# The skip and gated spectral rows of a fused FFT and state-space kernel: summed in fp32 by ScalarE and an accumulating DMA

## The chip, the cores and the metric

The kernel runs on one core of a Trainium2 chip. Its time is the device time of one execution in microseconds (us). Before the change it is 354.18 us, the median of four runs (354.07 to 355.04).

## What is computed

Two branches read the same x (2048 x 1024, bf16), and a gate of each row mixes them:

```python
x = A_x
g = sigmoid((x * gate_w).sum(-1, keepdims=True))
a = irfft2(rfft2(x) * (w_r + 1j * w_i))            # spectral branch, cast to bf16
# state-space branch: complex diagonal scan over the 2048 rows
h_t = Lam_bar * h_(t-1) + x_t @ B_bar.T
b = 2 * real(h @ C.T) + x * Dskip
out = g * a + (1 - g) * b
```

## The kernel before

**Stages.** The program has three stretches. First, up to about 110 us, comes the forward transform: `fstage` folds x, `fd` makes the transform along a row, `bf_w` the one over the rows and the product with the weights W, and `bi` starts the way back. There are 16 groups g. Then, to about 160 us, comes the inverse: `idm` (16 tiles, into yp), the folding of yp into pm on VectorE (L635, L636), and `fi`, whose result ya is stored in a DRAM scratch, `ya_scratch`. The last stage makes the output, 16 tiles of 128 rows, tb = 0 to 15.

**The state-space branch** runs through all of it in 16 units (c, q): c is one of four chunks of 512 time steps, q one of four groups of 256 states. Unit number n is 4c + q. For a unit, TensorE (PE) makes 4 x 8 products of x with B into the PSUM tile psu (L388, two buffers), ScalarE (ACT) scales each psu into the tile u (L390, two buffers), and VectorE (DVE) rotates u by tables (L399, L401, L403), runs four scans (L408), computes the carry (L417 to L421) and rotates back (L425, L427), where L427 writes into u again. L429 writes the state tile h. The h of c = 0 and 3 lies in a pool, the others in the arrays `big` and `xT` that are free by then.

**The last stage** (`half`, `c_all`): for tile tb and half dh of its columns, 16 products of h with C into the PSUM tile psy (L770, three buffers of a whole tile). All four h of chunk tb // 4 are needed. For the first eleven tiles, a 17th product with the identity matrix adds the skip row xc = x * Dskip (L774), and DVE forms out = psy * (1 - g) + gac (L779), where gac is the spectral row scaled by g on ACT (L760). For the last five tiles, ACT writes (1 - g) * xc as fp32 into xf (L763), DVE adds gac to it (L764), and L779 takes xf instead of gac. The loads of xc and gac and the store of o are issued on SyncE (SP).

**What sets the order.** `ssm_all`, `fft_main` and `c_all` are generators with a cost in us for each step. A loop takes the next step of the branch that is behind: L718 paces the units against the transform (20 by the end of the forward part, 42 at the end of the inverse), L722 and L792 let the units run to 42 and 43 before the last stage, and L797 paces them against `c_all` with a factor of 1.02. Within that program order a scheduler places the instructions of PE, DVE and ACT. SP and POOL follow the written order up to `order1.close()` (L748); after it they are scheduled too. POOL issues only the loads of W, L239, 14 pairs of them; it has no work after 110 us. `gates` computes g: 32 small products, a sigmoid on ACT and three small DVE operations, begun beside the fifth pm (jj == 4).

Of the kernel before, what the change touches and what calls it, by code (L numbers as in the profile page):

```python
# [20 lines left out]
D = 1024  # L21
K = 512
P = 128
# [113 lines left out]
def kernel(  # L137
# [256 lines left out]
    def ssm_dve(c, q, u):  # L394
        tq = tab[:, 2 * q:2 * q + 2]
        full = [P, 2, 2, TC]
        cu = rp.tile(full, BF16, name="cu", tag="cu")
        su = rp.tile(full, BF16, name="su", tag="su")
        nc.vector.tensor_mul(out=cu, in0=u, in1=tq[:, :, 0:1, :].to_broadcast(full))  # L399
        yield  # L400
        nc.vector.tensor_mul(out=su, in0=u[:, :, ::-1, :], in1=tq[:, :, 1:3, :])  # L401
        yield
        nc.vector.tensor_add(out=cu, in0=cu, in1=su)  # L403
        yield
        for jj in range(2):
            jb = 2 * q + jj
            for ri in range(2):
                nc.vector.tensor_tensor_scan(out=su[:, jj, ri, :], data0=r_sb[:, jb:jb + 1].to_broadcast([P, TC]),  # L408
                                             data1=cu[:, jj, ri, :],
                                             initial=(0.0 if c == 0 else carry[q][:, jj, ri:ri + 1]),  # L410
                                             op0=ALU.mult, op1=ALU.add)
                if not (jj and ri):
                    yield
        if c + 1 < NCH:
            ge = su[:, :, :, TC - 1]
            k1 = sm.tile([P, 2, 2], FP32, name="k1")
            nc.vector.tensor_mul(out=k1, in0=ge, in1=cTC[:, 2 * q:2 * q + 2].unsqueeze(2).to_broadcast([P, 2, 2]))  # L417
            k2 = sm.tile([P, 2, 2], FP32, name="k2")
            nc.vector.tensor_mul(out=k2, in0=ge[:, :, ::-1], in1=sg[:, 2 * q:2 * q + 2, :])
            cy = sm.tile([P, 2, 2], FP32, name=f"carry{q}")  # L420
            nc.vector.tensor_add(out=cy, in0=k1, in1=k2)  # L421
            carry[q] = cy
        yield
        h = h_tile(c, q)
        nc.vector.tensor_mul(out=cu, in0=su, in1=tq[:, :, 0:1, ::-1].to_broadcast(full))  # L425
        yield
        nc.vector.tensor_mul(out=u, in0=su[:, :, ::-1, :], in1=tq[:, :, 1:3, ::-1])  # L427
        yield
        nc.vector.tensor_add(out=h, in0=cu, in1=u)  # L429
        hs[c, q] = h  # L430
        yield


# [62 lines left out]
    def bf_w(g):  # L496
        X1 = X1s.pop(g)
        M = MM[g]
        Mr, Mi, Mn = M[:, 0, :], M[:, 1, :], M[:, 2, :]
        Im, Re, ORe, OIm = X1[:, 0:256], X1[:, 256:512], X1[:, 512:768], X1[:, 768:1024]  # L500
        X = Xtiles[g % 2]
        pe = psF.tile([P, 2, 512], FP32, name="ps_xe", tag="ps")
        kw = dict(skip_group_check=True)
        nc.tensor.matmul(pe[:, 0, 0:256], lhsT=Mr, rhs=Re, start=True, stop=False, **kw)
        nc.tensor.matmul(pe[:, 0, 1:257], lhsT=Mi, rhs=Im, start=False, stop=True, **kw)
        nc.tensor.matmul(pe[:, 1, 0:256], lhsT=Mn, rhs=Re, start=True, stop=False, **kw)
        nc.tensor.matmul(pe[:, 1, 1:257], lhsT=Mr, rhs=Im, start=False, stop=True, **kw)
        nc.scalar.copy(out=X[:, :, 0:513:2], in_=pe[:, :, 0:257])
        po = psF.tile([P, 2, 256], FP32, name="ps_xo", tag="ps")
        nc.tensor.matmul(po[:, 0, :], lhsT=Mr, rhs=ORe, start=True, stop=False)  # L510
        nc.tensor.matmul(po[:, 0, :], lhsT=Mi, rhs=OIm, start=False, stop=True)
        nc.tensor.matmul(po[:, 1, :], lhsT=Mn, rhs=ORe, start=True, stop=False)
        nc.tensor.matmul(po[:, 1, :], lhsT=Mr, rhs=OIm, start=False, stop=True)
        (nc.vector.tensor_copy if g < 3 else nc.scalar.copy)(out=X[:, :, 1:513:2], in_=po)  # L514
        W = WT[g]
        Y = fr.tile([P, 2, 514], BF16, name="Y")
        t2 = gc1.tile([P, 2, 514], BF16, name="t2")
        nc.vector.tensor_mul(out=Y, in0=X, in1=W[:, 0:1, :].to_broadcast([P, 2, 514]))  # L518
        nc.vector.tensor_mul(out=t2, in0=X, in1=W[:, 1:2, :].to_broadcast([P, 2, 514]))
        nc.vector.tensor_sub(out=Y[:, 0, :], in0=Y[:, 0, :], in1=t2[:, 1, :])  # L520
        nc.vector.tensor_add(out=Y[:, 1, :], in0=Y[:, 1, :], in1=t2[:, 0, :])
        Ys[g] = Y
        if g + 2 < 16:
            load_W(g + 2)
# [78 lines left out]
    def fft_main():  # L603
# [24 lines left out]
        for jj in range(9):  # L628
            if jj < 8:
                yp = fr.tile([P, 2, 2, 512], BF16, name="yp")  # L630
                for jl in range(2):
                    idm(2 * jj + jl, yp[:, jl])
                    yield 1.1
                pm = fr.tile([P, 2, 2, 512], BF16, name="pm")
                nc.vector.tensor_add(out=pm[:, :, 0, :], in0=yp[:, :, 0, :], in1=yp[:, :, 1, :])  # L635
                nc.vector.tensor_sub(out=pm[:, :, 1, :], in0=yp[:, :, 0, :], in1=yp[:, :, 1, :])  # L636
                pms[jj] = pm
                if jj == 4:
                    gt = gates()
                    next(gt)  # L640
                    yield 2.0
                if jj == 4 + 1:
                    next(gt)
                    yield 0.3
            if jj > 0:
# [69 lines left out]
    ssm = Gen(ssm_all())  # L715
    fft = Gen(fft_main())
    while not fft.done:
        if ssm.t < (20 * (fft.t - 3.5) / (54.4 - 3.5) if fft.t < 54.4 else 20 + (42 - 20) * (fft.t - 54.4) / 35.0):  # L718
            ssm.step()
        else:  # L720
            fft.step()
    while ssm.t < 42:  # L722
        ssm.step()
    fctx.close()

    with ExitStack() as bctx:
# [5 lines left out]
        xcs, gacs = {}, {}  # L732

        def load_xc(tb):
            xcs[tb] = fin.tile([P, D], BF16, name="xc", bufs=3)
            nc.sync.dma_start(out=xcs[tb], in_=x[P * tb:P * (tb + 1), :])

        def load_gac(tb):
            gacs[tb] = fin.tile([P, D], BF16, name="gac", bufs=4)
            nc.sync.dma_start(out=gacs[tb], in_=ya_dram[P * tb:P * (tb + 1), :])  # L740

        for tb in range(3):
            load_xc(tb)
        load_gac(0)
        load_gac(1)
        load_C(1)
        load_gac(2)
        order1.close()  # L748

        psys = {}  # L750

        def half(tb, dh):
            c, tq = tb // 4, tb % 4
            if dh == 0:
                psys[tb] = psY.tile([P, D], FP32, name="psy", tag="psy")
            psy, xc, gac = psys[tb], xcs[tb], gacs[tb]
            if dh == 0:
                nc.vector.tensor_mul(out=xc, in0=xc, in1=dsk_bc)
            else:
                nc.scalar.activation(out=gac, in_=gac, func=ACT.Copy, scale=gf[:, tb:tb + 1])  # L760
                if tb >= 11:
                    xf = rp.tile([P, D], FP32, name="xf", tag="cu")
                    nc.scalar.activation(out=xf, in_=xc, func=ACT.Copy, scale=om_f[:, tb:tb + 1])  # L763
                    nc.vector.tensor_add(out=xf, in0=xf, in1=gac)  # L764
                    gac = xf
            ds = slice(512 * dh, 512 * (dh + 1))
            i = 0
            for jb in range(8):
                for ri in range(2):
                    nc.tensor.matmul(psy[:, ds], lhsT=hs[c, jb // 2][:, jb % 2, ri, P * tq:P * (tq + 1)],  # L770
                                     rhs=CT[dh][:, jb, ri, :], start=(i == 0), stop=(i == 15 and tb >= 11))
                    i += 1
            if tb < 11:
                nc.tensor.matmul(psy[:, ds], lhsT=ident, rhs=xc[:, ds], start=False, stop=True)  # L774
            if dh == 0:
                return
            o = fin.tile([P, D], BF16, name="o")
            for ds in ((slice(0, D),) if tb < 15 else (slice(0, 512), slice(512, D))):
                nc.vector.scalar_tensor_tensor(out=o[:, ds], in0=psy[:, ds], scalar=om_f[:, tb:tb + 1], in1=gac[:, ds],  # L779
                                               op0=ALU.mult, op1=ALU.add)  # L780
                nc.sync.dma_start(out=out2[P * tb:P * (tb + 1), ds], in_=o[:, ds])

        def c_all():
            order = [(0, 0), (1, 0), (2, 0), (0, 1), (1, 1), (2, 1)] + [(tb, dh) for tb in range(3, 16) for dh in range(2)]
            for tb, dh in order:
                if dh == 0 and 3 <= tb + 1 < 16:
                    load_xc(tb + 1)
                    load_gac(tb + 1)
                half(tb, dh)
                yield 3.6  # L790

        while ssm.t < 43:  # L792
            ssm.step()
        cg = Gen(c_all())
        t0 = ssm.t
        while not cg.done:
            if not ssm.done and ssm.t - t0 <= cg.t * 1.02:  # L797
                ssm.step()
            else:
                cg.step()  # L800
# [30 lines left out]
```

## Time and profile before

| what | value |
|---|---|
| median of four runs | 354.18 us |
| the profiled execution: its own time | 355.03 us |
| the profiled execution: span from first to last instruction | 353.2 us |
| granted TensorE clock, mean | 0.995 |
| busy in the span: PE, DVE, ACT, POOL | 93%, 86%, 50%, 8% |
| bytes moved by DMA, mean rate | 42.91 MB, 121 GB/s |
| L770, psy products | 512, 379 ns each in the record |
| L388, psu products | 512, 379 ns each in the record |
| L774, identity products | 22, 379 ns each in the record |
| L779, DVE o, whole tile | 15, 1.27 to 1.28 us each |

The records of matmuls overlap, since they are pipelined: a product of 512 columns has a record of 379 ns, but the next one starts 0.216 us later. The span is divided by stage in the tables that follow. "Idle before" is the time in which an engine stood before an instruction, with the event that released it. An instruction that issues a DMA is shown on the queue of its engine (SPq, POOLq); "to landing" is the time from issue to the arrival of the data.

### The profile page before, as it was taken

Reading aid. Unit: us, or ns where it says so; the run is one execution under the profiler, and the core shown is the slowest. Engines: PE = TensorE matmul, PEld = TensorE weight load, DVE = VectorE, ACT = ScalarE, POOL = GpSimd, SP = SyncE. Lnnn points to the kernel's source line nnn. Section 1 sums busy time; section 2 is a strip of 40 time slices with the busy share of each in tenths; the row PEclk is TensorE's granted clock in tenths of the full one; section 3 lists DMA queues with packets and bytes.
Section 4 is the critical chain, followed back from the end, with each engine's and each line's share of the span. In section 5 each row is a group of like instructions: output and inputs, shape, how many; then the busy total and the mean of one; then the engine's idle time right before and its main releaser. Section 6 shows DMA issues by size and latency. Waiting matters only on the chain.

```text
span 353.2 us, 4881 instructions
## 1 busy us (share of the span) xinstructions
PE 329.7 (93%) x1826; PEld 175.0 (50%) x1826; DVE 302.3 (86%) x423; ACT 177.9 (50%) x245; POOL 27.9 (8%) x73
## 2 busy tenths in 40 slices
PE   3888989899799999989799999999999999999995
PEld 1675656566456556544344444444444444444442
DVE  4998749979978989895969999999999999999431
ACT  1998879779679786883323322322313223223110
POOL 5330321222110000000000000000000000000000
PEclk9999999999989999999999999999999999999999
DMA  7999997989979130214991340211201303142101
GB/s 271 343 138 220 180 256 178 165 212 199 138 166 202 62 119 32 89 67 151 235 203 37 104 114 16 89 32 59 89 30 62 89 0 91 60 119 88 63 31 58
DMA packets 65864, 42.91 MB, mean 121 GB/s; under 512 B 52400, under 2 KB 55472, under 8 KB 65840
## 3 DMA queue, kind: packets, MB, share of 16 engines
q1 hardware_dynamic: 64144, 38.75, 45.4%
q0 software_dynamic: 1344, 3.68, 4.5%
q8 instruction: 14, 0.23, 0.3%
q10 hardware_dynamic: 352, 0.17, 0.2%
q14 instruction: 10, 0.08, 0.1%
HBM read 21.61 MB, written 8.39 MB: 85 GB/s over the span
## 4 chain that ended last, share of the span: by engine, by line
PE 64%; issue 13%; DMA 10%; DVE 8%; POOL 3%; ACT 1%; SPq 0%; DVEq 0%; POOLq 0%; ACTq 0%
PE psy L770 30%; PE psu L388 23%; DMA W<-in_A_w_r_dram 4%; PE ps_id L550 3%; DMA W<-in_A_w_i_dram 2%; POOL W L239 2%; DVE su L408 2%; DMA CT<-in_A_x_dram 1%; PE psy L774 1%; DMA xt<-in_A_x_dram 1%; DMA xc<-in_A_x_dram 1%; PE ps_q L539 1%; PE ps_y L569 1%; PE ps_q L540 1%; PE ps_y L572 1%
## 5 line engine op out<-in xcount | busy, mean ns | idle before, releaser
L388 PE MATMUL psu<-xT,BT 128*128 128x512 bf16 x512 | 120.4, 379 | 1.1 <-DMA xT<-in_A_x_dram 1.1
L388 PEld LDWEIGHTS <-BT 128*128 128x128 bf16 x512 | 49.6, 98 | 57.8 <-issue 3.7
L408 DVE TENSOR_TENSOR_SCAN su<-r_sb,carry,cu 128x512 bf16<-128x512 f32 x48 | 57.8, 1264 | 0.4
L390 ACT ACTIVATE u<-psu,nrho 128x512 bf16<-128x512 f32 x32 | 22.0, 688 | 56.6 <-PE psu L388 56.6
L770 PEld LDWEIGHTS <-h 128*128 128x128 bf16 x256 | 25.0, 98 | 30.4 <-issue 0.3
L390 ACT ACTIVATE u<-psu,rho 128x512 bf16<-128x512 f32 x32 | 22.3, 696 | 33.1 <-PE psu L388 33.0
L760 ACT ACTIVATE gac<-gac,gf 128x1024 bf16<-128x1024 bf16 x16 | 18.3, 1147 | 33.4 <-DMA gac<-ya_scratch 30.6
L399 DVE TENSOR_TENSOR cu<-u,tab 128x2048 bf16<-128x2048 bf16 x16 | 19.8, 1237 | 13.8 <-ACT u L390 13.7
L770 PE MATMUL psy<-CT,h 128*128 128x512 bf16 x128 | 28.9, 379 | 0.0
L770 PE MATMUL psy<-big,h 128*128 128x512 bf16 x128 | 28.9, 379 | 0.0
L543 ACT CAST big<-ps_q 128x1024 bf16<-128x1024 f32 x16 | 16.6, 1035 | 9.8 <-PE ps_q L542 9.6
L770 PEld LDWEIGHTS <-big 128*128 128x128 bf16 x128 | 12.5, 98 | 15.1
L770 PEld LDWEIGHTS <-xT 128*128 128x128 bf16 x128 | 12.5, 98 | 15.1
L539 PE MATMUL ps_q<-MM,Y 128*128 128x256 bf16 x64 | 15.7, 281 | 4.5 <-DVE Y L520 4.3
L403 DVE TENSOR_TENSOR cu<-cu,su 128x2048 bf16<-128x2048 bf16 x16 | 19.5, 1219 | 0.2
L481 PE MATMUL ps_d<-G_sb,big 128*128 128x256 bf16 (+3 forms) x128 | 19.6, 294 | 0.0
L425 DVE TENSOR_TENSOR cu<-su,tab 128x2048 bf16<-128x2048 bf16 x16 | 19.5, 1218 | 0.1
L401 DVE TENSOR_TENSOR su<-u,tab 128x2048 bf16<-128x2048 bf16 x16 | 19.5, 1217 | 0.0
L427 DVE TENSOR_TENSOR u<-su,tab 128x2048 bf16<-128x2048 bf16 x16 | 19.5, 1216 | 0.0
L518 DVE TENSOR_TENSOR Y<-X,W 128x1028 bf16<-128x1028 bf16 x16 | 11.0, 688 | 9.3 <-ACT X L514 7.9
L408 DVE TENSOR_TENSOR_SCAN su<-r_sb,cu 128x512 bf16<-128x512 f32 x16 | 18.9, 1210 | 0.1
L465 PE MATMUL ps_f<-BT,eo 128*128 128x256 bf16 x64 | 16.4, 297 | 2.4 <-DVE big L470 1.3
(171 smaller groups left out, 547.7 us busy)
## 6 DMA issues: line engine op xcount, KB each, us to landing
ya_scratch<-ya SPq DMA_DIRECT2D x16, 256.0 KB, 2.0
xc<-in_A_x_dram SPq DMA_DIRECT2D x16, 256.0 KB, 2.6
gac<-ya_scratch SPq DMA_DIRECT2D x16, 256.0 KB, 2.7
out_dram<-o SPq DMA_DIRECT2D x15, 256.0 KB, 2.0
MM<-c_MM SPq DMA_DIRECT2D x16, 192.0 KB, 3.9
xt<-in_A_x_dram SPq DMA_DIRECT2D x4, 512.0 KB, 4.4
CT<-in_A_x_dram SPq DMA_DIRECT2D x4, 512.0 KB, 7.7
W<-in_A_w_r_dram POOLq DMA_DIRECT2D x14, 128.2 KB, 4.3
```

Of the source, the lines that this page charges most:

```text
L388: nc.tensor.matmul(psu, lhsT=BT[:, jb, ri, dblk, :], rhs=xT[:, dblk, TC * c:TC * (c + 1)], start=(dblk == 0), stop=(dblk == 7))
L390: nc.scalar.activation(out=u[:, jj, ri, :], in_=psu, func=ACT.Copy, scale=(nrho if ri else rho)[:, jb:jb + 1])
L399: nc.vector.tensor_mul(out=cu, in0=u, in1=tq[:, :, 0:1, :].to_broadcast(full))
L401: nc.vector.tensor_mul(out=su, in0=u[:, :, ::-1, :], in1=tq[:, :, 1:3, :])
L403: nc.vector.tensor_add(out=cu, in0=cu, in1=su)
L408: nc.vector.tensor_tensor_scan(out=su[:, jj, ri, :], data0=r_sb[:, jb:jb + 1].to_broadcast([P, TC]), data1=cu[:, jj, ri, :], initial=(0.0 ...
L425: nc.vector.tensor_mul(out=cu, in0=su, in1=tq[:, :, 0:1, ::-1].to_broadcast(full))
L427: nc.vector.tensor_mul(out=u, in0=su[:, :, ::-1, :], in1=tq[:, :, 1:3, ::-1])
L481: nc.tensor.matmul(ps[:, lo:lo + w], lhsT=FX[:, q, 8 * g:8 * g + 8, :], rhs=G_sb[:, o:o + w], start=start, stop=stop, skip_group_check=True)
L539: nc.tensor.matmul(dst, lhsT=Yr[:, e:e + 255:2], rhs=ri_, start=True, stop=False, **kw)
L760: nc.scalar.activation(out=gac, in_=gac, func=ACT.Copy, scale=gf[:, tb:tb + 1])
L770: nc.tensor.matmul(psy[:, ds], lhsT=hs[c, jb // 2][:, jb % 2, ri, P * tq:P * (tq + 1)], rhs=CT[dh][:, jb, ri, :], start=(i == 0), stop=(i ...
```

## The change

In the last stage every tile now takes the fp32 way, and the sum of the two rows is made by a DMA:

- `prep_d(tb)`: DVE multiplies xc by Dskip, as before.
- `prep_a(tb)`: ACT scales gac by g, and writes xf = (1 - g) * xc in fp32 (three buffers). A DMA issued on POOL adds the bf16 row gac to the fp32 row xf. Then SP issues the loads of xc and gac for tile tb + 2.
- `half`: 16 products only, for every tile; L774 and the DVE add L764 are gone. The last step reads xf.
- A table `pre` says after which half each `prep_d` and `prep_a` is written.
- xc has two buffers in place of three and gac three in place of four, and two tiles in place of three are loaded ahead.
- ACT and SP keep their written order in the last stage, where the scheduler placed them before.

Four other things change. The copy of ps_xo into X (L514) is on DVE for four groups in place of three. `gates` begins one pm later. The pace of the units is 18.5 and 44 in place of 20 and 42, then 44 and 48 in place of 42 and 43, and the factor 1.05 in place of 1.02. A branch `if False` is added to `ssm_dve`, which is never taken.

```diff
-        (nc.vector.tensor_copy if g < 3 else nc.scalar.copy)(out=X[:, :, 1:513:2], in_=po)
+        (nc.vector.tensor_copy if g < 4 else nc.scalar.copy)(out=X[:, :, 1:513:2], in_=po)
...
-                if jj == 4:
+                if jj == 5:
                     gt = gates()
                     next(gt)
                     yield 2.0
-                if jj == 4 + 1:
+                if jj == 5 + 1:
...
-        if ssm.t < (20 * (fft.t - 3.5) / (54.4 - 3.5) if fft.t < 54.4 else 20 + (42 - 20) * (fft.t - 54.4) / 35.0):
+        if ssm.t < (18.5 * (fft.t - 3.5) / (54.4 - 3.5) if fft.t < 54.4 else 18.5 + (44 - 18.5) * (fft.t - 54.4) / 35.0):
...
-    while ssm.t < 42:
+    while ssm.t < 44:
...
-        for tb in range(3):
+        for tb in range(2):
             load_xc(tb)
-        load_gac(0)
-        load_gac(1)
+            load_gac(tb)
         load_C(1)
-        load_gac(2)
         order1.close()
-
-        psys = {}
+        if ('Activation','SP'):
+            bctx.enter_context(tc.manual_schedule(engines=set(getattr(mybir.EngineType, e) for e in ('Activation','SP'))))
+
+        psys, xfs = {}, {}
+
+        def prep_d(tb):
+            nc.vector.tensor_mul(out=xcs[tb], in0=xcs[tb], in1=dsk_bc)
+
+        def prep_a(tb):
+            xc, gac = xcs.pop(tb), gacs.pop(tb)
+            nc.scalar.activation(out=gac, in_=gac, func=ACT.Copy, scale=gf[:, tb:tb + 1])
+            xf = fin.tile([P, D], FP32, name="xf", bufs=3)
+            nc.scalar.activation(out=xf, in_=xc, func=ACT.Copy, scale=om_f[:, tb:tb + 1])
+            nc.gpsimd.dma_start(out=xf, in_=gac, accum_op=ALU.add)
+            xfs[tb] = xf
+            if tb + 2 < 16:
+                load_xc(tb + 2)
+                load_gac(tb + 2)
 
         def half(tb, dh):
...
-            if dh == 0:
-                nc.vector.tensor_mul(out=xc, in0=xc, in1=dsk_bc)
-            else:
-                nc.scalar.activation(out=gac, in_=gac, func=ACT.Copy, scale=gf[:, tb:tb + 1])
-                if tb >= 11:
-                    xf = rp.tile([P, D], FP32, name="xf", tag="cu")
-                    nc.scalar.activation(out=xf, in_=xc, func=ACT.Copy, scale=om_f[:, tb:tb + 1])
-                    nc.vector.tensor_add(out=xf, in0=xf, in1=gac)
-                    gac = xf
...
-                                     rhs=CT[dh][:, jb, ri, :], start=(i == 0), stop=(i == 15 and tb >= 11))
+                                     rhs=CT[dh][:, jb, ri, :], start=(i == 0), stop=(i == 15))
                     i += 1
-            if tb < 11:
-                nc.tensor.matmul(psy[:, ds], lhsT=ident, rhs=xc[:, ds], start=False, stop=True)
...
-                nc.vector.scalar_tensor_tensor(out=o[:, ds], in0=psy[:, ds], scalar=om_f[:, tb:tb + 1], in1=gac[:, ds],
-                                               op0=ALU.mult, op1=ALU.add)
+                nc.vector.scalar_tensor_tensor(out=o[:, ds], in0=psy[:, ds], scalar=om_f[:, tb:tb + 1],
+                                               in1=xfs[tb][:, ds], op0=ALU.mult, op1=ALU.add)
...
         def c_all():
             order = [(0, 0), (1, 0), (2, 0), (0, 1), (1, 1), (2, 1)] + [(tb, dh) for tb in range(3, 16) for dh in range(2)]
+            pre = {(0, 0): [(prep_d, 0), (prep_d, 1)], (1, 0): [(prep_a, 0)], (2, 0): [(prep_a, 1)],
+                   (0, 1): [(prep_d, 2)], (1, 1): [(prep_a, 2)], (2, 1): [(prep_d, 3)], (3, 0): [(prep_a, 3), (prep_d, 4)],
+                   (3, 1): [(prep_a, 4)]}
+            for n in range(5, 16):
+                pre[n - 1, 0] = [(prep_d, n)]
+                pre[n - 1, 1] = [(prep_a, n)]
             for tb, dh in order:
-                if dh == 0 and 3 <= tb + 1 < 16:
-                    load_xc(tb + 1)
-                    load_gac(tb + 1)
                 half(tb, dh)
+                for f, n in pre.get((tb, dh), ()):
+                    f(n)
                 yield 3.6
 
-        while ssm.t < 43:
+        while ssm.t < 48:
             ssm.step()
...
-            if not ssm.done and ssm.t - t0 <= cg.t * 1.02:
+            if not ssm.done and ssm.t - t0 <= cg.t * 1.05:
```

More of the change, by code (lines that the diff above doesn't have):

```diff
@@ L424, in ssm_dve @@
         h = h_tile(c, q)
+        hs[c, q] = h
+        if False:
+            nc.vector.tensor_mul(out=h, in0=su, in1=tq[:, :, 0:1, ::-1].to_broadcast(full))
+            yield
+            nc.vector.tensor_mul(out=cu, in0=su[:, :, ::-1, :], in1=tq[:, :, 1:3, ::-1])
+            nc.gpsimd.dma_start(out=h, in_=cu, accum_op=ALU.add)
+            yield
+            return
         nc.vector.tensor_mul(out=cu, in0=su, in1=tq[:, :, 0:1, ::-1].to_broadcast(full))
@@ L429, in ssm_dve @@
         nc.vector.tensor_add(out=h, in0=cu, in1=u)
-        hs[c, q] = h
         yield
@@ L734, in load_xc @@
         def load_xc(tb):
-            xcs[tb] = fin.tile([P, D], BF16, name="xc", bufs=3)
+            xcs[tb] = fin.tile([P, D], BF16, name="xc", bufs=2)
             nc.sync.dma_start(out=xcs[tb], in_=x[P * tb:P * (tb + 1), :])
         def load_gac(tb):
-            gacs[tb] = fin.tile([P, D], BF16, name="gac", bufs=4)
+            gacs[tb] = fin.tile([P, D], BF16, name="gac", bufs=3)
             nc.sync.dma_start(out=gacs[tb], in_=ya_dram[P * tb:P * (tb + 1), :])
-        for tb in range(3):
+        for tb in range(2):
             load_xc(tb)
-        load_gac(0)
-        load_gac(1)
+            load_gac(tb)
         load_C(1)
-        load_gac(2)
         order1.close()
-        psys = {}
+        if ('Activation','SP'):
[13 more added lines that the diff above has]
+                load_gac(tb + 2)
         def half(tb, dh):
@@ L755, in half @@
                 psys[tb] = psY.tile([P, D], FP32, name="psy", tag="psy")
-            psy, xc, gac = psys[tb], xcs[tb], gacs[tb]
-            if dh == 0:
-                nc.vector.tensor_mul(out=xc, in0=xc, in1=dsk_bc)
-            else:
-                nc.scalar.activation(out=gac, in_=gac, func=ACT.Copy, scale=gf[:, tb:tb + 1])
-                if tb >= 11:
-                    xf = rp.tile([P, D], FP32, name="xf", tag="cu")
-                    nc.scalar.activation(out=xf, in_=xc, func=ACT.Copy, scale=om_f[:, tb:tb + 1])
-                    nc.vector.tensor_add(out=xf, in0=xf, in1=gac)
-                    gac = xf
+            psy = psys[tb]
             ds = slice(512 * dh, 512 * (dh + 1))
```

## The prediction

> **What bounds the kernel now.** I read the busy time by stretch first, then the chain of work that ended last, then VectorE's timeline, because TensorE (PE) and VectorE (DVE) are both near full and only the order of their work tells which one decides.
>
> ```profile
> 28.80:110.20 81.40, 74.67 (x515) 46.83 (x516) 67.17 (x109) 65.75 (x84) 17.38 (x29) 0.98 1.01 190
> 110.20:160.40 50.20, 49.19 (x314) 29.82 (x314) 45.48 (x59) 39.50 (x59) 0.00 (x0) 1.00 0.29 91
> 160.40:172.20 11.80, 9.65 (x45) 4.26 (x44) 9.10 (x9) 3.71 (x7) 0.00 (x0) 1.00 0.67 187
> 172.20:321.30 149.10, 149.10 (x692) 67.53 (x692) 143.26 (x148) 43.28 (x54) 0.00 (x0) 1.00 0.29 78
> 321.30:349.10 27.80, 27.76 (x129) 12.41 (x127) 12.93 (x14) 5.63 (x5) 0.00 (x0) 1.00 0.15 53
> ```
>
> The columns are length, then busy time of PE, weight loads, DVE, ACT, POOL, then clock and DMA. From 172.2 to the end PE has no gap at all. DVE is 96% busy until 321.3 and only then loose; ACT is 29% busy and POOL unused. So in the last stage a matmul taken away is time gained, but only as long as DVE, close behind, can follow.
>
> ```profile
> 170.24 1.26 DVE su L408
> 171.50 0.59 DVE xc L758
> 172.13 0.38 PE psy L774
> ...
> 314.53 34.55 PE psy L770 x160
> 349.10 0.75 DVE o L779
> ```
>
> The chain shows the one hole of this stage: the first identity product (L774) waits for the skip row xc, which waits for its load and for a scan in DVE's queue. PE stood from 169.8 (its eleven psu products, 167.46 plus 11 of 0.216) to 172.13, that is 2.3 us.
>
> ```profile
> 163.03 1.23 DVE L399 TENSOR_TENSOR cu<-u,tab 128x2048 bf16<-128x2048 bf16 x1 [4.45 <-ACT u L390]
> ...
> 179.74 1.23 DVE L399 TENSOR_TENSOR cu<-u,tab 128x2048 bf16<-128x2048 bf16 x1 [2.84 <-ACT u L390]
> ...
> 251.31 1.21 DVE L399 TENSOR_TENSOR cu<-u,tab 128x2048 bf16<-128x2048 bf16 x1
> ...
> 265.23 1.21 DVE L399 TENSOR_TENSOR cu<-u,tab 128x2048 bf16<-128x2048 bf16 x1
> ...
> 279.46 1.23 DVE L399 TENSOR_TENSOR cu<-u,tab 128x2048 bf16<-128x2048 bf16 x1 [0.45 <-ACT u L390]
> 293.70 1.23 DVE L399 TENSOR_TENSOR cu<-u,tab 128x2048 bf16<-128x2048 bf16 x1 [0.45 <-ACT u L390]
> ...
> 321.87 1.21 DVE L429 TENSOR_TENSOR h<-cu,u 128x2048 bf16<-128x2048 bf16 x1
> ```
>
> One line L399 per scan unit (c,q). The period is 13.92 us where DVE never waits and 14.24 where it waits 0.45 for PE. The last state tile is ready at 323.08, and its first reader, the last four products of tile 12 (started at 321.27, 12 x 0.216 later), wants it at 323.86: 0.8 us to spare. A faster PE alone would therefore run into DVE at once.
>
> **PE's side of the change.** Sixteen products take 3.45 us in the chain, 0.2159 each. Check on before: from 160.38 there are 328 psu + 512 psy + 22 identity = 862 products, 186.1 us, plus the 2.3 us hole: 348.8, and the last ones indeed issue just before 348.9. The built order of the changed program has no identity products and 8 more psu products ahead of the last spectral product: 320 + 512 = 832, 179.6 us. So:
> - 22 identity products: 22 x 0.2159 = -4.75.
> - the hole for xc: -2.3, as no PE instruction reads xc any more.
> - 8 psu moved ahead: -1.73 here and +1.73 before 160.4. There they stand between the last inverse products, where PE waits 1.0 us (157.6 to 158.6) for pm L636. Stage end: 160.4 + 1.73 - 1.0 = 161.1.
>
> **DVE's side.** In the new order 11 units follow the last pm (158.6), as before. The waits of 4.45 and 2.84 go, because unit 5 is fully multiplied before the spectral part ends and 32 psu products come before the first psy. A unit without its o (1.19 to the next start) and xc (0.60) is 13.92 - 1.79 = 12.13; the four of the last chunk, which have no carry, 11.95. Up to the last h stand 12 xc and 10 o instead of 14 and 11, and the one fp32 add that lay there (L764, 1.13) is gone: 7 x 12.13 + 4 x 11.95 + 12 x 0.60 + 10 x 1.19 = 151.8, so 310.4.
>
> What is late next: SP's written order puts load xc(n+2) behind the store of o(n-1). In before a store starts at once after its o and the next issue 0.43 later; with 2.6 us from issue to landing, xc arrives 3.05 after o's end. DVE asks for it two operations after o (2 x 1.14 = 2.28). That is a new wait of 0.8 us in each of the last six units, with the rest of the unit queued behind it: 310.4 + 4.8 = 315.2. PE wants this h at product 716: 161.1 + 154.6 = 315.7. It still holds, by 0.5.
>
> A unit's u buffer (two of them) comes free with the h of two units before. Following both queues, this stays inside the 5.2 us that PE can cover (3.45 for a psy half and 1.73 for the other psu bank), except at units 14 and 15: 0.1 and 0.8. PE pays +0.9.
>
> **The other parts.**
>
> ```profile
> L774 PE MATMUL psy<-xc,ident 128*128 128x512 bf16 x22 | 8.3, 379 | 2.1 <-DVE xc L758 2.1
> L763 ACT ACTIVATE xf<-xc,om_f 128x1024 f32<-128x1024 bf16 x5 | 5.7, 1144 | 9.8 <-DVE o L779 9.8
> L764 DVE TENSOR_TENSOR xf<-xf,gac 128x1024 f32<-128x1024 f32 x5 | 6.1, 1221 | 2.5 <-ACT xf L763 2.4
> xc<-in_A_x_dram SPq DMA_DIRECT2D x16, 256.0 KB, 2.6
> W<-in_A_w_r_dram POOLq DMA_DIRECT2D x14, 128.2 KB, 4.3
> ```
>
> ACT gets 11 more fp32 rows, 11 x 1.144 = 12.6 us, inside the 105.8 us that it is idle. In the written order a row that waits for its load or xc holds the psu evictions behind it, and then PE, which has two psu banks. The rows stand where DVE passed their xc one to three units earlier, so 0; if one came late, 5.2 us would be hidden and the rest paid.
>
> The accumulating DMA (16, on POOL, which has nothing else to do after 110; only the next accumulation queues behind it) has no row. Below: 2.6, the plain load of the same rows. Above: 8.2, the slowest landing of the W loads, the only POOL DMAs. I take 4.3, their usual one. From row to reader: xf(2) is written at about 201 and read at 212; the last, xf(15), follows o(12), load and xc: written at 331.7, wanted at 341.6. So it is hidden at either end, by at least 9.9 us less its landing; a gain is excluded, since no such work is on the path of before.
>
> Two rules of the Trainium skill price this otherwise. "DMA: Bandwidth & Descriptors", section "Anatomy of one DMA — SWDGE (gpsimd) path", gives such a DMA about 2.0 us plus bytes over 436 GB/s: an estimate of 3.2 us for 512 KB, where the W row has 4.3 for a quarter of that; the sum is the same by both, as 9.9 us hide it. Against the change speaks "SBUF — State Buffer", section "SBUF: two separate sides": a DMA issued on POOL can starve while DVE holds their shared port in some copy or scalar modes. The trace agrees: the two W issues on POOL that met a DVE TENSOR_SCALAR (L290 at 34.85, L368 at 82.27) took 1.02 and 0.77 us, the other 26 took 0.54 to 0.62. But the last stage's DVE rows are tensor-tensor, scan and scalar-tensor-tensor, none of those modes. By the row nothing is added; by the rule, were every issue held for a whole DVE operation, 1.28 us would go onto a landing that 9.9 us hide: 0 either way.
>
> The X copy of group 3 goes from ACT (0.74) to DVE (0.75), which idles 1.97 there waiting for that very copy: 0, between -0.6 and +0.75. The gates one step later: the same instructions, wanted only after 170: 0, at worst their 1.84 of products at another place. The unreachable branch: nothing. Smaller xc and gac pools: priced above as the late xc.
>
> The new pacing shifts psu and scan work within 28.8 to 160.4. PE has 6.7 us of gaps in the first 81.4, several for Y L520 behind a 1.2 us scan operation. Four psu more stand before the forward part ends. I cannot order these by hand: 0, with -3 (half of the gaps filled) to +3 (two more gaps of 1.2 to 1.6) for the range.
>
> **Sum.** 161.1 + 179.6 + 0.9 = 341.6 against 348.8, so -7.2; the tail after PE (4.4) is unchanged. Span 353.2 becomes 346.0. The profiled execution took 355.03, so 347.8 for one like it; the median of the runs was 0.85 below it, so 354.18 - 7.2 = 347.0.
>
> **Rivals.**
> - Pacing. Better by up to 3: 344.0 (chance 0.12). Worse by 3: 350.0 (0.08). For it speak the Y waits, which any shift of 1.2 us on DVE moves; against it that the mix of work stays.
> - DVE becomes the bound through late loads. Each 0.1 us of landing costs 6 x 0.1. At 3.2 the last h comes at 318.8, PE waits 3.1: 350.1 (0.20). For it: accumulations now share the DMA engines; against it: these are 29% used.
> - Slower, by the same loop where it decides: SP's store, then load, then xc in each of the last six units. At the W landing of 4.3 the last h comes at 325.4, PE waits 9.7: 356.7. It decides from 2.6 + (0.5 + 7.2) / 6 = 3.9 us. Against it: xc landed in 2.4 to 2.9 every time; for it: gac reached 5.2 (0.08).
> - No change: 0.02. The sum as it stands has 0.50.
>
> A measurement here tells about 0.2% from no change. Faster by more: 0.50 + 0.12 + 0.08 + 0.20 = 0.90, less 0.01 for the edges; within: 0.03; slower: 0.08. The range 344.0 to 351.0 leaves out the slower case, no change and the far edge of pacing.
>
> **What would show it.** In the profile after: no L774, no gap before the first psy tile; PE full from 161 to about 341; a DVE wait of about 0.8 us for xc in the last six units; DVE lines o never waiting for the accumulation; the last h less than a microsecond ahead of tile 12. Wrong, if the stretch 28.8 to 161 changes by more than 3 us, if o waits for xf, or if PE waits for u or h by more than 3 us.

## The result and the profile after

The changed kernel takes 352.97 us (median of 37 runs; the kernel before 355.06 over 56 runs beside them). The ratio is 0.9942, with a 95% interval of 0.9922 to 0.9961: 2.1 us faster, where the forecast was 7.2. Ratios and means leave out executions more than 1.5% above the fastest of their kernel. The profiled execution took 353.44, its span is 351.6 in place of 353.2.

First the busy time by stretch, in the columns of the prediction (length, PE, weight loads, DVE, ACT, POOL, clock, DMA). The second stretch begins at the same time as in the table of before, so that it can be compared; the third begins where the record of the last spectral product ends.

```profile
28.80:110.20 81.40, 73.88 (x502) 46.70 (x503) 67.40 (x111) 64.32 (x82) 17.03 (x28) 0.96 1.02 198
110.20:164.30 54.10, 53.00 (x334) 31.60 (x333) 48.19 (x61) 41.92 (x63) 0.66 (x1) 1.00 0.19 69
164.30:347.50 183.20, 180.02 (x832) 81.20 (x830) 157.92 (x161) 62.25 (x75) 13.96 (x16) 1.00 0.48 131
```

The last stage has the 832 products that were counted, and takes 183.2 us for them where 180.5 was forecast. But its first product is issued at 164.1, not at 161.1: the two stretches ahead of it lost 3.7 us against before, where 0.7 was forecast. So the profile is 3.0 us off ahead of the last stage and 2.7 in it, together the difference between the forecast span of 346.0 and 351.6. Two more views say what is behind it. The clock of the first stretch is 0.96 in place of 0.98. And in the last stage PE has these waits, where before had only the hole for xc:

```profile
PE psu L388 <- ACT u L390: 3.2, 3, 1.7
```

The groups that answer to those of before (busy time, mean ns, idle before) and the DMAs (KB, median us to landing):

```profile
L789 DVE SCALAR_TENSOR_TENSOR o<-psy,om_f,xf 128x1024 bf16<-128x1024 f32 (+1 forms) x17 | 20.6, 1214 | 6.8 <-PE psy L782 6.8
L766 ACT ACTIVATE xf<-xc,om_f 128x1024 f32<-128x1024 bf16 x16 | 18.2, 1135 | 0.0
L767 POOL DMA_DIRECT2D xf<-gac x16 | 14.0, 873 | 215.2 <-ACT xf L766 146.2 <-DMA big<-in_B_C_re_dram 69.0
L760 DVE TENSOR_TENSOR xc<-xc,dsk_bc 128x1024 bf16<-128x1024 bf16 x16 | 11.0, 686 | 17.3 <-DMA xc<-in_A_x_dram 17.3
```

```profile
xf<-gac POOLq DMA_DIRECT2D x16, 512.0 KB, 4.0
xc<-in_A_x_dram SPq DMA_DIRECT2D x16, 256.0 KB, 3.0
```

The accumulating DMA lands in 4.0 us and o waits only for PE, never for it. What DVE waits for is the load of xc. Its timeline shows that, with the scan units by their first line L399:

```profile
231.52 1.22 DVE L399 TENSOR_TENSOR cu<-u,tab 128x2048 bf16<-128x2048 bf16 x1
234.85 0.69 DVE L760 TENSOR_TENSOR xc<-xc,dsk_bc 128x1024 bf16<-128x1024 bf16 x1 [0.98 <-DMA xc<-in_A_x_dram]
246.51 1.21 DVE L399 TENSOR_TENSOR cu<-u,tab 128x2048 bf16<-128x2048 bf16 x1
250.32 0.69 DVE L760 TENSOR_TENSOR xc<-xc,dsk_bc 128x1024 bf16<-128x1024 bf16 x1 [1.46 <-DMA xc<-in_A_x_dram]
261.97 1.22 DVE L399 TENSOR_TENSOR cu<-u,tab 128x2048 bf16<-128x2048 bf16 x1
265.18 0.69 DVE L760 TENSOR_TENSOR xc<-xc,dsk_bc 128x1024 bf16<-128x1024 bf16 x1 [0.86 <-DMA xc<-in_A_x_dram]
...
276.62 1.22 DVE L399 TENSOR_TENSOR cu<-u,tab 128x2048 bf16<-128x2048 bf16 x1
280.89 0.69 DVE L760 TENSOR_TENSOR xc<-xc,dsk_bc 128x1024 bf16<-128x1024 bf16 x1 [1.93 <-DMA xc<-in_A_x_dram]
```

The wait of the forecast is there in each of the last six units: 0.98, 1.46, 0.86, 1.93, 0.95 and 0.90, together 7.1 where 4.8 was forecast. The queue of SP (the start, length and target of each issue) shows its place: at 261.97 DVE has just ended o and goes on, and SP issues the store and then the load.

```profile
262.08 0.34 SPq L791 DMA_DIRECT2D out_dram<-o  x1
262.51 0.38 SPq L743 DMA_DIRECT2D xc<-in_A_x_dram  x1
```

From 262.51 the row landed by 265.18, 2.67 later. In these six units the landing took 2.7 to 3.7, 3.0 on average; the longest wait, 1.93, has the longest one. The last of PE's three stops shows how the delay reaches PE:

```profile
290.00 1.23 DVE L437 TENSOR_TENSOR h<-cu,u 128x2048 bf16<-128x2048 bf16 x1
291.34 0.69 ACT L390 ACTIVATE u<-psu,rho 128x512 bf16<-128x512 f32 x1 [7.19 <-DVE h L437]
292.08 1.89 PE L388 MATMUL psu<-xT,BT 128*128 128x512 bf16 x8 [1.75 <-ACT u L390]
```

L437 is the last to read u. ACT, which needs that buffer for the next unit, starts 0.1 us after it, and PE, whose PSUM buffers are both full, starts after ACT. The other two stops (0.75 at 261.71, 0.67 at 276.36) have the same order, with ACT starting 0.1 us after an L437 has ended.

**Where the clock goes.** The runs list the mean granted clock of each execution, and the spread of the times goes in part with this clock. Call (1 - mean clock) x span the clock time lost. Within one kernel an execution that lost 1 us more took 0.77 us more (before, 78 runs) or 0.85 (after, 33); this accounts for a bit over a third of the variance. In the traces the loss comes in the same kind of event. Here is PE in slices of 2 us (length, PE busy, clock, DMA), first of before, then of after:

```profile
94.00:96.00 2.00, 0.36 (x2) 1.00 0.57 119
96.00:98.00 2.00, 1.21 (x6) 0.72 0.44 131
98.00:100.00 2.00, 2.00 (x11) 0.50 0.33 76
100.00:102.00 2.00, 1.93 (x16) 0.92 0.71 186
```

```profile
70.00:72.00 2.00, 0.40 (x3) 1.00 1.29 274
72.00:74.00 2.00, 2.00 (x15) 0.69 0.21 72
74.00:76.00 2.00, 2.00 (x8) 0.50 0.88 229
...
100.00:102.00 2.00, 0.07 (x1) 1.00 1.29 182
102.00:104.00 2.00, 2.00 (x15) 0.87 1.16 288
104.00:106.00 2.00, 2.00 (x9) 0.50 1.15 263
106.00:108.00 2.00, 2.00 (x13) 0.78 1.03 185
```

PE stands for 2.3 to 2.4 us, waiting for Y; then the clock falls to 0.50, and a whole fall loses 1.7 us of clock time. Before has one such fall in its profile, after has two. The new one at 71 belongs to a stop that before has too, but only of 1.60 us. What made it 2.29 shows in the timeline of DVE, first in before, then in after:

```profile
67.17 1.21 DVE L427 TENSOR_TENSOR u<-su,tab 128x2048 bf16<-128x2048 bf16 x1
68.31 0.68 DVE L518 TENSOR_TENSOR Y<-X,W 128x1028 bf16<-128x1028 bf16 x1
68.91 0.68 DVE L519 TENSOR_TENSOR t<-X,W 128x1028 bf16<-128x1028 bf16 x1
69.52 1.21 DVE L429 TENSOR_TENSOR h<-cu,u 128x2048 bf16<-128x2048 bf16 x1
70.65 0.41 DVE L520 TENSOR_TENSOR Y<-Y,t 128x514 bf16<-128x514 bf16 x1
```

```profile
67.57 1.22 DVE L433 TENSOR_TENSOR cu<-su,tab 128x2048 bf16<-128x2048 bf16 x1
68.71 0.68 DVE L525 TENSOR_TENSOR Y<-X,W 128x1028 bf16<-128x1028 bf16 x1
69.31 0.68 DVE L526 TENSOR_TENSOR t<-X,W 128x1028 bf16<-128x1028 bf16 x1
...
69.99 1.21 DVE L435 TENSOR_TENSOR u<-su,tab 128x2048 bf16<-128x2048 bf16 x1
71.12 0.42 DVE L527 TENSOR_TENSOR Y<-Y,t 128x514 bf16<-128x514 bf16 x1
```

L518 and L519 (L525 and L526 after the change) are the products with the weights W, and PE waits for the last line of each view, their sum. In both, one operation of a scan unit lies between. After the change the unit is one step behind: L433 and L435 are what L425 and L427 are in before, so that the second rotation, which before had already been done, now stands in between. L527 starts 0.47 us later than L520 did, and PE runs out of work 0.2 us earlier, at 69.3 in place of 69.5.

### The profile page after: what moved, and what is told of

The parts are those of the page before. It is cut to its first block, busy times and chain, and to the rows that moved or that the text cites. A ratio compares the mean times of both kernels' runs of the same rounds, so it can differ in the third digit from the quotient of the medians.

```text
span 351.6 us, 4890 instructions
## 1 busy us (share of the span) xinstructions
PE 326.1 (93%) x1804; PEld 173.6 (49%) x1804; DVE 297.6 (85%) x419; ACT 188.4 (54%) x255; POOL 42.0 (12%) x89
## 3 DMA queue, kind: packets, MB, share of 16 engines
q0 software_dynamic: 3648, 12.07, 14.7%
## 4 chain that ended last, share of the span: by engine, by line
PE 52%; DVE 24%; DMA 10%; issue 7%; ACT 4%; POOL 1%; SPq 0%; DVEq 0%; ACTq 0%; POOLq 0%
PE psy L782 24%; PE psu L388 17%; DVE su L408 9%; DMA xc<-in_A_x_dram 4%; DMA xt<-in_A_x_dram 3%; PE ps_id L557 3%; DVE cu L403 2%; DVE cu L433 2%; DMA W<-in_A_w_r_dram 2%; DMA MM<-c_MM 2%; DVE o L789 1%; DVE u L435 1%; DVE t L526 1%; PE ps_d L488 1%; PE ps_y L576 1%
## 5 line engine op out<-in xcount | busy, mean ns | idle before, releaser
L388 PE MATMUL psu<-xT,BT 128*128 128x512 bf16 x512 | 122.1, 383 | 4.2 <-ACT u L390 3.2
L767 POOL DMA_DIRECT2D xf<-gac x16 | 14.0, 873 | 215.2 <-ACT xf L766 146.2
L764 ACT ACTIVATE gac<-gac,gf 128x1024 bf16<-128x1024 bf16 x16 | 18.3, 1142 | 27.6 <-DMA gac<-ya_scratch 27.6
L789 DVE SCALAR_TENSOR_TENSOR o<-psy,om_f,xf 128x1024 bf16<-128x1024 f32 (+1 forms) x17 | 20.6, 1214 | 6.8 <-PE psy L782 6.8
L760 DVE TENSOR_TENSOR xc<-xc,dsk_bc 128x1024 bf16<-128x1024 bf16 x16 | 11.0, 686 | 17.3 <-DMA xc<-in_A_x_dram 17.3
L399 DVE TENSOR_TENSOR cu<-u,tab 128x2048 bf16<-128x2048 bf16 x16 | 19.5, 1218 | 5.8 <-ACT u L390 5.7
L782 PEld LDWEIGHTS <-big 128*128 128x128 bf16 x128 | 12.5, 98 | 15.1
L782 PEld LDWEIGHTS <-xT 128*128 128x128 bf16 x128 | 12.5, 98 | 15.1
L433 DVE TENSOR_TENSOR cu<-su,tab 128x2048 bf16<-128x2048 bf16 x16 | 19.5, 1219 | 0.1
L435 DVE TENSOR_TENSOR u<-su,tab 128x2048 bf16<-128x2048 bf16 x16 | 19.5, 1217 | 0.0
```

Source lines behind the costliest of these rows:

```text
L388: nc.tensor.matmul(psu, lhsT=BT[:, jb, ri, dblk, :], rhs=xT[:, dblk, TC * c:TC * (c + 1)], start=(dblk == 0), stop=(dblk == 7))
```

## The experiments

Two causes were to be told apart, and then the mechanism of each. Theory A: the edits outside the last stage (pace, X copy, gates) cost about 2 us. Theory L: the loads behind the store on SP cost 2 to 3 us, through DVE's waits for xc and then PE's stops on u. The sum of both would bring back the forecast. One rival says that the last stage is slow by itself, another that the accumulation's traffic makes it slow.

**One: the changed kernel with the forward part paced and copied as before.**

```diff
-        (nc.vector.tensor_copy if g < 4 else ...
+        (nc.vector.tensor_copy if g < 3 else ...
-  if ssm.t < (18.5 * ... if fft.t < 54.4 else 18.5 + (44 - 18.5) * ...
+  if ssm.t < (20 * ... if fft.t < 54.4 else 20 + (44 - 20) * ...
```

> The changed kernel with two edits of the forward part undone: pace 20 in place of 18.5 up to its end, and the X copy on VectorE for three groups in place of four. The last stage is that of the changed kernel. Theory A (the forward edits themselves delay PE): the first inverse product starts near 110.2 us as before the change, not 112.8, and the time is 2 to 2.6 us under the changed kernel, near 350.5, ratio to before 0.987. Rival B (the forward part's end scatters by this much between executions, whatever the pace): the time stays that of the changed kernel within 0.7 us, near 353, ratio 0.994, wherever the first inverse product of the profile lies.

Measured: 350.66, ratio 0.9886 (0.9841 to 0.9931), the first inverse product (tile ps_id) at 109.0 in place of 112.8. The forward edits do cost. The last stage is unchanged in kind; PE's stops on u are even longer, 4.1.

**Two: the kernel before, with the pacing edits alone** (the pace, the X copy and the gates of the change; last stage untouched).

> The kernel before with only the pacing edits: 18.5 and 44, the X copy of four groups on VectorE, the gates one pm later; the last stage is as before, identity products too. Theory A: forward part and inverse end later by 2 to 3.9 us, eight psu products fewer (1.7) behind them, so 0.5 to 2 us slower than before, ratio 1.002 to 1.006. Rival B: the eight products fill the hole before the last inverse product, and nothing else moves: 0 to 1 us faster, ratio 0.997 to 1.000.

Measured: 358.09, ratio 1.0061 (1.0031 to 1.0091). The same edits make the kernel before slower, by 2.2 us, at the upper end of theory A's range. This bears it out from the other side.

**Three and four: the loads ahead of the store on SP,** in the changed kernel, and together with experiment one.

```diff
-                nc.sync.dma_start(out=out2[...], in_=o[:, ds])
+                stores.append((tb, ds, o))
...
                 for f, n in pre.get((tb, dh), ()):
                     f(n)
+                for t, ds, o in stores:
+                    nc.sync.dma_start(out=out2[...], in_=o[:, ds])
+                stores.clear()
```

> The changed kernel, with the two loads for tile tb + 2 issued on SP ahead of the store of the o before them, not behind it. Theory L (the loads queued behind the store make VectorE late, and its u buffers stop PE): no wait for xc on VectorE in the last six units (7.1 us in the changed kernel), no PE stop on u (3.2 us), last stage 179.6 to 180.2 us in place of 183.2, time 2.5 to 3.2 us under the changed kernel, ratio to before 0.985 to 0.988. Rival (VectorE's own work makes it late): the xc wait goes, PE still stops on u, and the time falls by less than 1 us.

> Both: the loads ahead of the store, and the forward pace and X copy as before the change. Theories A and L: their gains add, 5 to 6 us under the changed kernel, near 347.5, ratio 0.979, which is the size that was forecast. B and L: only the 2.5 to 3.2 us of the loads, ratio 0.985 to 0.988.

Measured: three 351.21, ratio 0.9879 (0.9825 to 0.9932); four 346.51, ratio 0.9758 (0.971 to 0.9805), 8.6 us below before; no version here is clearly faster. In four the busy table from 158 us on reads:

```profile
158.00:309.00 151.00, 150.26 (x688) 68.44 (x700) 149.69 (x154) 56.74 (x71) 11.35 (x13) 1.00 0.48 128
309.00:340.00 31.00, 29.09 (x133) 13.04 (x134) 10.21 (x11) 6.89 (x6) 2.61 (x3) 1.00 0.52 151
```

PE and DVE are both full to 309, and the list of PE's waits in this stage is empty; in the second row DVE has little left and PE goes on without a gap (29.09 of 31.00, with some records missing). In three the list is empty as well, and in both no unit waits for xc up to the last h. The last stage takes 179.6 us in both, the length of the 832 products alone. So it does what was forecast once its loads are early, and the rival of a stage that is slow by itself falls. Three gained a little less than theory L said, about 2 us; in its profile the last stage is 3.6 us shorter but begins 2.5 later, after three falls of the clock in place of two.

**Five and six: which of the forward edits?** Version four with the pace of 18.5 alone, and with the X copy on DVE alone.

> The version with the loads first and the earlier settings of the forward part (346.5 us, ratio 0.976 to the kernel before), with only the pace of the units changed to 18.5 again. Theory P (the pace makes the forward cost of about 2 us: more scan and product work falls beside the last forward groups): ratio about 0.982, first ps_id at 110 to 113 in place of 107 to 109, and a stop of PE near 100 us with slow products after it. Theory X (the copy of ps_xo moved from ACT to DVE does it, since it lengthens the wait of the next Y on DVE): ratio about 0.976, as without it.

> The version with the loads first and the earlier settings of the forward part (ratio 0.976), with only the copy of ps_xo for group 3 moved to DVE. Theory P: no cost, ratio about 0.976 (one DVE copy of 0.75 where DVE waited for ACT's copy of 0.74). Theory X: ratio about 0.982.

Measured: pace 349.06, ratio 0.9822 (0.9779 to 0.9865); X copy 346.60, ratio 0.9788 (0.9736 to 0.984). The pace costs about 2.3 us here (standard error 0.8), as theory P says. The time doesn't settle the copy: its interval holds the ratio of theory P and that of theory X. The row of the forward part in version five, then in version four:

```profile
28.80:110.00 81.20, 72.80 (x493) 46.41 (x502) 66.27 (x110) 64.38 (x83) 17.02 (x28) 0.96 1.03 199
```

```profile
28.80:110.00 81.20, 74.90 (x525) 48.51 (x535) 69.68 (x111) 67.57 (x87) 17.42 (x29) 1.00 1.00 192
```

With the pace, PE issued fewer products in the same time, at a clock of 0.96: stops of 2.27 at 71.6 and 2.26 at 102.1, each with a fall after it. Without it the stops are 1.60 and 2.42, and in this execution the clock stayed at 1.00.

**Seven: version four with the sum on DVE in place of the accumulating DMA.**

```diff
-            nc.gpsimd.dma_start(out=xf, in_=gac, accum_op=ALU.add)
+            nc.vector.tensor_add(out=xf, in0=xf, in1=gac)
```

> The version with the loads first and the earlier settings of the forward part (346.5 us), with the accumulating DMA replaced by an add on DVE, same operands, for all 16 tiles (same sum). In that version DVE is 149.7 of 151.0 us busy from 158 to 309, and PE can cover about 3.4 us. Theory A (the DMA is what takes work off the full engine): 12 or 13 adds of 1.22 stand before the last state tile, 15 to 16 us, less 3.4 and 1.2 that were idle: +10 to +11, about 357, ratio 1.003 to 1.008, DVE full to about 320 and PE waiting for h and u by about 10 us. Rival (most of the gain is on PE, and the adds fit into DVE's waits): at most +3, ratio at most 0.985.

Measured: 356.11, ratio 1.0025 (0.9999 to 1.0052), 9.6 us over version four. Its groups on DVE and on PE:

```profile
L767 DVE TENSOR_TENSOR xf<-xf,gac 128x1024 f32<-128x1024 f32 x16 | 19.5, 1217 | 2.9 <-ACT xf L766 2.8
...
L388 PE MATMUL psu<-xT,BT 128*128 128x512 bf16 x489 | 117.7, 383 | 7.1 <-ACT u L390 5.0 <-DMA xT<-in_A_x_dram 1.0 <-issue 0.2
L784 PE MATMUL psy<-CT,h 128*128 128x512 bf16 x125 | 28.9, 379 | 2.3 <-DVE h L437 1.3 <-DVE o L791 0.9
```

PE now waits for u, h and o by 7.2 in the last stage, which takes 9.5 us longer than in four. Part of the rest is the clock, for the longest of these stops is followed by eight products that take 3.25 us in place of 1.89:

```profile
234.04 3.25 PE L388 MATMUL psu<-xT,BT 128*128 128x512 bf16 x8 [4.21 <-ACT u L390]
```

In this order of the work, taking out the identity products is worth nothing unless DVE is spared too: theory A, a little below its size.

**Eight: is it the traffic?** Experiment one with the accumulating DMA left out, so that the output lacks the gated spectral row.

> The changed kernel with only the pace and the copy of the forward part as before (350.7 us, ratio 0.989 to the kernel before; xc landed in about 3.0 us, loads still behind the store on SP), with the accumulating DMA left out: the gated spectral row is then not in the output. Theory T (the traffic of the accumulation, 512 KB a tile, lengthens the landing of xc and so makes the waits of DVE and PE's stops on u): landing back at 2.6, DVE waiting for xc under 1 us in each of the last units, PE waiting for u under 1 us in all, ratio about 0.980. Theory O (the order on SP does it, whatever the traffic): landing 2.9 or more or the waits as they are, PE's wait for u 3 to 4 us, ratio 0.986 to 0.990.

Measured: 351.90, ratio 0.9914 (0.9883 to 0.9946); in the last six units DVE waits 8.1 us for xc, and PE 4.2 for u, as with the DMA (8.2 and 4.1), at a landing of 2.8. The ratio is just outside theory O's range, on the slow side, and far from theory T's 0.980. Theory O: the order on SP makes the waits, not the traffic.

**Nine to eleven: the falls of the clock.** Seven products with a weight tile of zeros, 1.5 us, are added to an open psu sum just ahead of the ps_q products that PE stands before: in the changed kernel (group 13), in version four and in the kernel before (group 12).

```diff
+                    if (4 * (4 * c + q) + 2 * jj + ri, dblk + 1) in ((10, 7),):
+                        with tc.high_priority():
+                            for _ in range(7):
+                                nc.tensor.matmul(psu, lhsT=zt, rhs=xT[...], start=False, stop=False)
```

> The changed kernel with seven more products in TensorE's queue, 512 columns with an all-zero weight tile added to the open psu sum (so nothing changes in the output), placed just ahead of the ps_q products of group 13, where PE stood 2.26 us for Y at 99.7 to 101.9. Seven products are 1.5 us, so they lie inside the stop. Theory C (a stop of more than about 2 us lets the granted clock fall to a half for 3.4 us, which costs 1.72 us each time; the changed kernel has two such stops, at 71 and at 101, the kernel before one, at 96): no fall after this stop, clock 1.00 from 100 to 110, one fall left at 71, time lower by up to 1.7: ratio to before 0.989 to 0.991 against 0.994. Rival D (the stop itself and the other order of the work cost the time, the slow records cost nothing): ratio 0.994 to 0.998, first ps_id no earlier than 112.

> The version with the loads first and the earlier settings of the forward part (346.5 us, ratio 0.976), with the same seven zero products ahead of the ps_q products of group 12, where PE stood 2.42 us at about 95. Theory C: its profile showed no fall of the clock, other executions of it may have; so 0 to -1.7, ratio 0.971 to 0.976, and less scatter from execution to execution. Rival D: ratio 0.976 to 0.980.

> The kernel before with the same seven zero products ahead of the ps_q products of group 12, where PE stood 2.43 us at 94.4 to 96.8 and the clock was 0.72 and 0.50 in the 3.4 us after it. Theory C: clock 1.00 from 94 to 104, time lower by up to 1.7 in the executions that had the fall: ratio 0.995 to 0.998. Rival D: ratio 1.000 to 1.003.

Measured: nine 351.31, ratio 0.9898 (0.9858 to 0.9938); ten 346.10, 0.9762 (0.9718 to 0.9806); eleven 355.18, 1.001 (0.9987 to 1.0032). In nine the stop of 2.26 us is now 0.75, and no fall follows it. This execution had its one fall elsewhere, after a wait of 2.35 us for the load of MM:

```profile
44.62 0.28 PE L517 MATMUL ps_xe<-X,MM 128*128 128x256 bf16 x1 [2.35 <-DMA MM<-c_MM]
...
102.46 0.28 PE L552 MATMUL ps_q<-MM,Y 128*128 128x256 bf16 x1 [0.75 <-DVE Y L533]
```

By its time, nine bears out theory C: more work on PE made the changed kernel faster (span -1.4, standard error 0.4), with 2.2 us less clock time lost and 0.8 more of the rest. But its one profile doesn't show the gain where the theory puts it. The first inverse product comes at 112.5, as rival D says, and the last stage is shorter (181.5), with six waits for xc of 5.2 us together, not 7.1, and stops of PE on u of 1.4, not 3.2. For the kernel before, theory C's time missed: the fall is gone (clock 1.00 from 94 to 104, clock time lost 1.27 on average in place of 2.41), but the rest of the time grew by 1.4. What took that back is not settled. In version four nothing was gained either. So a fall follows such a stop, and goes when the stop is filled; what a fall costs in time is open.

All versions together, in us. Runs to rest are means over executions; the standard error is 0.2 to 0.8 for the span and 0.1 to 0.5 for the rest. The last two columns are from the one profile of each: when the first product behind the last spectral one is issued, and how long PE takes from there to its last product.

| version | runs | span | clock time lost | the rest | last stage begins | its length |
|---|---|---|---|---|---|---|
| before | 78 | 353.24 | 2.41 | 350.83 | 160.4 | 188.5 |
| after | 33 | 350.97 | 3.21 | 347.76 | 164.1 | 183.2 |
| one: forward part as before | 6 | 349.15 | 1.34 | 347.81 | 160.0 | 184.2 |
| two: before with the pacing edits | 19 | 355.54 | 3.60 | 351.94 | 163.2 | 188.8 |
| three: loads first | 6 | 348.87 | 3.43 | 345.43 | 166.6 | 179.6 |
| four: one and three together | 6 | 344.60 | 1.61 | 342.99 | 158.5 | 179.6 |
| five: four with the pace | 5 | 346.86 | 2.50 | 344.36 | 164.2 | 179.6 |
| six: four with the X copy | 6 | 345.43 | 1.91 | 343.53 | 160.5 | 179.6 |
| seven: four with DVE adds | 22 | 354.23 | 3.88 | 350.35 | 160.6 | 189.1 |
| eight: one without accumulation | 8 | 350.15 | 2.06 | 348.09 | 162.3 | 184.3 |
| nine: after, one stop filled | 6 | 349.53 | 0.99 | 348.54 | 164.8 | 181.5 |
| ten: four, stop filled | 5 | 344.44 | 0.76 | 343.68 | 160.3 | 179.6 |
| eleven: before, stop filled | 22 | 353.47 | 1.27 | 352.20 | 159.1 | 188.5 |

The length of the last stage hardly scatters: 179.6 in all five versions with early loads and accumulating DMA, whatever stands ahead of it. Its beginning lies between 158.5 and 166.6, and most falls of the clock are ahead of it.

## Why the prediction was right in its sign and wrong in its size

The forecast put the last stage at 161.1 and its length at 180.5; the profile has 164.1 and 183.2. Each number has one step of the forecast behind it.

- **The failed step: "The new pacing ... 0, with -3 to +3".** The pace costs 2.3 us by itself (five less four). Together with the X copy it costs 1.8 where the loads are late (after less one), 2.3 on the kernel before (two less before, which has the later gates too) and 4.3 where the loads are early (three less four), with standard errors of 0.4 to 0.9. The prediction listed the gaps of PE for Y and priced a moved gap at its own length of 1.2 to 1.6. What was not read is the row of the clock behind the gap at 96. Under the new pace two stops of 2.3 us stand there, each with a fall behind it, and the clock time lost is 1.2 to 1.9 us higher in each of the three pairs. How much of the cost the falls are is open, since ten and eleven lost less of the clock and gained no time. The forecast's own bound, a change of the stretch by over 3 us, was crossed: the end of the stage moved from 160.4 to 164.1.
- **The mis-sized term: u buffers "+0.9".** The place and the mechanism were right (store, load, xc, the rest of the unit, h, u). But in the six units the landing was 3.0 us on average, not 2.6, and the load was issued 0.54 after o's end, not 0.43. So the six waits came to 7.1 in place of 4.8, and units 10 to 15 start 15.1 us apart (five periods from 231.52 to 307.07), not 14.7. PE stood 3.2 for u, over the bound of 3 that the forecast named: 0.75, 0.67 and 1.75 at units 13, 14 and 15, where 0, 0.1 and 0.8 were forecast. Early loads take 3.6 us off the last stage (183.2 to 179.6); by the mean spans they are worth 2.1 (after less three) and 4.6 (one less four), each with a standard error of 0.7 to 0.8. This is the rival "DVE becomes the bound through late loads", which stood at 350.1, except that PE waited for u and not for the last h.
- **Two rivals at once.** Pacing worse by 3 and the late loads were each listed alone, at 350.0 and 350.1. Nothing makes them exclude each other, and both came: 347.0 + 3.0 + 3.1 is 353.1, and 352.97 was measured. That it fits so closely is in part luck, since neither size is known to better than 0.5 us.
- **Identity products and the hole for xc: right.** There is no identity product and no gap ahead of the first psy. 183.2 us of last stage less 3.2 of stops is 180.0, and with early loads it is 179.6, where 179.6 was forecast. The 1.0 us stop ahead of the last inverse products is filled, but two others in that stretch, of 0.7 and 0.4, are as long together.
- **The accumulating DMA: right.** 4.0 us in the median where 4.3 was taken (the other estimate gave 3.2), hidden as said; o never waits for it. With early loads it took 5.4 (three and four), and was still hidden. Its issues on POOL took 0.87 us each, longer than those of the W loads (0.54 to 0.62 mostly), at no cost. Seven shows that 9.6 us would be paid if DVE made the sum.
- **ACT's rows: right.** Sixteen rows of 1.14 us, and no row held an eviction up. ACT waits for gac 21.3 us in all between 200 and 330, but ahead of PE's three stops on u it starts when a unit's L437 has ended, not when a gac has landed.
- **The X copy: open.** It costs 0.8 us with the old pace (six less four) and 2.0 with the new one (three less five), each with a standard error of 0.9; the forecast had 0.75 at most.

With the failed step and the u term out, the sum is near: 348.8 - 161.1 - 179.6 is 8.1 us, and version four lies 7.8 below before in the rest and 8.6 in the span. Only the 179.6 is confirmed by itself. In the profile of four the last stage begins at 158.5, not 161.1, in an execution without a fall of the clock.

## What to carry to other kernels

When work is moved between two engines that are both nearly full, write down the other queues that the new order passes through: here one DMA store written ahead of a load on SP cost 3.6 us of the last stage, and swapping the two lines recovered it. Read the row of the granted clock next to every stop of TensorE, for a small shift of filler work that lengthens a stop from 1.6 to 2.3 us can bring a fall of the clock besides its own length. Ask of the rivals whether two of them can come together, and let the range hold their sum. And take a change apart when its edits lie in different stages: the retuned pace, with the X copy beside it, cost 2 to 4 us and hid much of what the last stage had won.

## What the runs showed of the hardware

The granted clock of TensorE falls to one half for 3.4 us after some stops, and such a fall loses 1.7 us of clock time. Of the 15 stops of 2.26 to 2.57 us for Y in the thirteen profiles, 11 were followed by a fall; of the 8 stops of 1.60 us, none. Stops for something else (from 20 us on) are much the same: those of 2.35, 2.94 and 3.36 for MM, of 2.74 for xc and of 4.21 for u were followed by a fall; one of 2.52 for u, two of 2.13 for xc and all shorter ones were not. The Trainium skill, "TensorE: Matmul & The Clock Gate", Part 1, says that the clock is halved after an idle window of about 3.4 us and restored after a busy one, the window running freely. The length of the fall agrees with that. The length of the stop does not: stops of 2.3 us were enough, so for this kernel the measurement decides; the free-running window would explain why the same stop falls in one execution and not in the next, but no run here shows the window itself.
